# A pre-norm attention and feed-forward kernel: nine bf16 products of constant ones as the warm-up, and the epsilon constant set by GpSimd

## The chip, the core and the metric

The kernel runs on one core of one Trainium2 chip. The metric is the time of one execution in device microseconds, lower is better. The core has a matrix engine (TensorE, PE in the profile; its weight loads are shown apart as PEld), three engines for elementwise work (VectorE or DVE, ScalarE or ACT, GpSimd or POOL), and a queue engine (SyncE, SP) that here issues nearly all DMA transfers.

## What is computed

One transformer block on 2048 tokens of 1024 features: a layer norm, sliding-window attention with 32 heads, a residual, a second layer norm, a SiLU feed-forward of width 3584, a residual. Inputs and output are bf16.

```
def _A_ref(x, wqkv, wo):
    B, S, D = x.shape
    H = 32; Dh = D // H; W = 256
    qkv = (lambda x, *d: x.transpose(*d))((x @ wqkv).reshape(B, S, 3, H, Dh), 2, 0, 3, 1, 4)
    ...
    mask = (idx[:, None] - idx[None, :] >= 0) & (idx[:, None] - idx[None, :] < W)
    ...
def _B_ref(x, w1, w2):
    h = _silu(jnp.einsum("bsd,df->bsf", x, w1))
    return jnp.einsum("bsf,fd->bsd", h, w2)

h = x + _A_ref(_layernorm(x, axis=-1), A_wqkv, A_wo)
h2 = h + _B_ref(_layernorm(h, axis=-1), B_w1, B_w2)
```

## The kernel before

The tokens are worked in four blocks of 512, each block in four tiles of 128 tokens. On-chip memory is cut by hand into a few regions (`r_w` weights and the transposed normed tokens, `r_o` the ring of token tiles, `r_a` queries, keys, values and later activations, `r_e` scratch and the attention probabilities). The order of instructions on each engine is the order in which the program writes them (`tc.manual_schedule()`); the tile framework adds the semaphores. After the opening, TensorE goes through value, query and key products for block 0, then the same products of each later block with the attention of the block before woven in, then the output projection, then the feed-forward. The change touches only the first microseconds, which run as follows.

**Preamble.** GpSimd sets four one-element-per-partition constants of the runtime (line 749 in the profile), among them `const-bfloat16-1.0`; then all engines pass a common start.

**Constants (lines 147 to 153).** VectorE clears `warm`, a 128x128 f32 patch at the start of `r_e`, and sets `eps`, one f32 in each partition. ScalarE's first work is a square root of `eps` into `dummy`; it brings in the table of the square root, and nothing reads its result. Because that instruction reads `eps`, ScalarE's queue stands at it until `eps` is there.

**Loads (lines 155 to 163).** SP issues token tile 0 (`load_x(0, 0)`, 256 KB). ScalarE issues token tile 1 (`load_x(0, 1, nc.scalar)`), right behind the square root in its queue. SP then issues the first 512 value columns of the weights in four parts of 256 KB (`load_wqkv(2 * D, 4)`, line 145; part n holds row blocks 2n and 2n+1 of the eight that a product sums over), then token tiles 2 and 3 and the other columns.

**Identity and ones column (lines 165 to 167).** GpSimd builds `ident`, the 128x128 identity for transposes on TensorE (a memset and an affine select inside `make_identity`), and then sets the column of ones beside the values in `r_a`.

**Warm-up (lines 170 to 176).** TensorE multiplies the zeros of `warm` by themselves, once over 512 and once over 384 columns, in f32, into the bank `o_ps[0]`. Nothing reads the result. Each shows as two weight loads and two products in the trace.

**First tokens (lines 463 to 498).** For tiles 0 and 1, ScalarE takes the mean of one half (`half_mean`, line 467), VectorE that of the other (469); VectorE subtracts the mean (`center`, 474) in four pieces; TensorE transposes pairs of 128x128 pieces (`turn_first`, 224), ScalarE (VectorE for some of tile 1) copies them from PSUM (227), and TensorE multiplies them with the value weights (497). The list `ORDER` fixes the sequence on TensorE: transposes (0,0), (0,1), (0,2) of tile 0, products with row blocks 0 and 1, transpose (0,3), products with row blocks 2 and 3, transpose (1,0), products with 4 and 5, and so on. ScalarE's queue holds the half means of tile 0 and tile 1 first and the copies of the transposes behind them. `eps` is read again by later square roots (lines 215, 482) and by the exponential that brings in its table (544).

Of the kernel before, what the change touches and what calls it, by code (L numbers as in the profile page):

```python
# [8 lines left out]
BF16 = mybir.dt.bfloat16  # L9
F32 = mybir.dt.float32  # L10
# [4 lines left out]
P = 128  # L15
N_HEADS = 32
WINDOW = 256
LN_EPS = 1e-5
# [30 lines left out]
def kernel(  # L49
# [10 lines left out]
    nc = tc.nc  # L60
# [15 lines left out]
    const = ctx.enter_context(tc.tile_pool(name="const", bufs=1))  # L76
# [13 lines left out]
    r_e = big.tile([P, 13312], BF16, name="r_e")  # L90
# [5 lines left out]
    o_ps = [ps.tile([P, 8, 64], F32, name=f"o_ps{i}") for i in range(2)]  # L96
    acc_ps = [ps.tile([P, 512], F32, name=f"acc{i}") for i in range(2)]

    def view(region, off, *dims):
        n = 1  # L100
        for d in dims:
            n *= d
        ap = region[:, off:off + n]
        if len(dims) == 2:
            return ap.rearrange("p (a b) -> p a b", b=dims[1])
        if len(dims) == 3:
            return ap.rearrange("p (a b c) -> p a b c", b=dims[1], c=dims[2])
        return ap
# [35 lines left out]
        for k in range(0, KT, n):  # L144
            queues[k // n % len(queues)].dma_start(out=dst[:, k:k + n, :], in_=wqkv_v[:, k:k + n, c0:c0 + 512])

    warm = view(r_e, 0, 2 * P).bitcast(F32)
    nc.vector.memset(warm, 0.0)

    eps = const.tile([P, 1], F32, name="eps")  # L150
    nc.vector.memset(eps[:], LN_EPS)
    dummy = const.tile([P, 1], F32, name="dummy")
    nc.scalar.activation(out=dummy[:], in_=eps[:], func=ACT.Sqrt)

# [7 lines left out]
            load_x(0, 3)  # L162
    load_wqkv(0)

    ident = const.tile([P, P], BF16, name="ident")
    make_identity(nc, ident[:])
    nc.gpsimd.memset(v[:, :, :, DH:VW], 1.0)


    wide = bass.AP(tensor=warm.tensor, offset=warm.offset, ap=[warm.ap[0], [0, 4], warm.ap[1]])  # L170

    def busy(n):
        nc.tensor.matmul(o_ps[0][:].rearrange("p (a c) b -> p a (c b)", c=2)[:, 0:n], lhsT=warm, rhs=wide[:, 0:n], start=True, stop=True)

    for n in (4, 3):
        busy(n)


    def ln_half(xt, stats, c):
# [399 lines left out]
    for g0 in range(0, G, 4):  # L579
        for w in range(2):  # L580
            for g in range(g0, g0 + 4):
                qk_group(0, w, g, dve if g % 2 else act)
                n = g0 * 2 + w * 4 + g % 4
# [105 lines left out]
    for b in range(NB):  # L689
# [4 lines left out]
        for ft in range(FT):  # L694
# [8 lines left out]
            if b == 0 and 7 <= ft < 15:  # L703
                j, c = divmod(ft - 7, 2)
# [60 lines left out]
```

## Time and profile before

| | us |
|---|---|
| median of three runs | 692.42 |
| the three runs | 692.87, 690.78, 692.42 |
| the profiled execution | 692.34 |
| its span, first to last instruction | 690.5 |
| TensorE busy in the span | 675.9 |
| VectorE, ScalarE, GpSimd busy | 291.8, 244.0, 160.6 |

The span leaves out 692.34 - 690.5 = 1.84 us before the first and behind the last instruction. In a timeline, each line gives start, length, engine, source line, operation, output and input, how many instructions are merged, and in brackets how long the engine sat idle before and what ended that. A product's shown length contains its drain, so the distance from start to start is what a product costs in a row of them.

### The profile page before, as it was taken

What the parts mean: (1) busy time and instruction counts of PE and PEld (TensorE: products, weight loads), DVE (VectorE), ACT (ScalarE), POOL (GpSimd) and SP (SyncE); (2) the same over time, 40 slices, a digit from 0 to 9 for tenths busy, and PEclk for the clock granted to TensorE, in tenths of its full rate; (3) what the DMA queues carried; (4) which work ended last, traced back from release to release, by engine and by line L of the source; (5) the groups of instructions that cost most, each with busy time, mean ns of one, the idle gap of its engine ahead of it and who ended that gap; (6) DMA issues with size and microseconds to landing.
All of it is one profiled execution on the core that took longest, in us unless ns stands there. A gap on an engine that the chain in (4) does not pass through costs nothing.

```text
span 690.5 us, 14116 instructions
## 1 busy us (share of the span) xinstructions
PE 675.9 (98%) x5890; PEld 341.8 (50%) x6004; DVE 291.8 (42%) x614; ACT 244.0 (35%) x465; POOL 160.6 (23%) x295
## 2 busy tenths in 40 slices
PE   9999999999999999999999999999999999999998
PEld 4445555555555555544444444444444444444445
DVE  5267647744444449443316133343133251333111
ACT  6326666666667666421310033300133100233000
POOL 1006666566666656500000000000000000000000
DMA  8832141136241879970023310022300024100110
GB/s 263 270 57 76 39 86 56 25 64 184 72 131 24 257 219 270 229 266 31 32 84 108 92 39 0 1 91 70 85 0 1 24 88 94 39 1 1 30 39 24
DMA packets 78640, 61.48 MB, mean 89 GB/s; under 512 B 52464, under 2 KB 62704, under 8 KB 78576
## 3 DMA queue, kind: packets, MB, share of 16 engines
q1 hardware_dynamic: 78432, 60.31, 31.4%
q8 instruction: 47, 0.77, 0.5%
q10 hardware_dynamic: 144, 0.26, 0.1%
q14 instruction: 17, 0.14, 0.1%
HBM read 39.85 MB, written 8.39 MB: 70 GB/s over the span
## 4 chain that ended last, share of the span: by engine, by line
PE 94%; DMA 2%; DVE 2%; issue 1%; SPq 0%; DVEq 0%
PE hacc L675 19%; PE acc L259 16%; PE hacc L712 14%; PE acc L712 14%; PE acc L675 9%; PE acc L249 6%; PE o_ps L392 5%; PE acc L280 4%; PE sc L312 2%; PE hacc L280 1%; DMA r_a<-h_dram 1%; PE sc L364 1%; DMA h_dram<-r_t 1%; DMA r_w<-in_A_wqkv_dram 1%; DVE ln_st L180 1%
## 5 line engine op out<-in xcount | busy, mean ns | idle before, releaser
L382 POOL TENSOR_SCALAR_AFFINE_SELECT r_e<-r_e 128x512 bf16<-128x512 bf16 (+1 forms) x288 | 157.6, 562 | 125.7 <-ACT r_e L372 61.1
L712 PEld LDWEIGHTS <-r_a 128*128 128x128 bf16 x952 | 90.7, 98 | 103.1
L675 PEld LDWEIGHTS <-r_w 128*128 128x128 bf16 x896 | 87.2, 98 | 105.0
L675 PE MATMUL hacc<-r_e,r_w 128*128 128x512 bf16 x468 | 104.9, 379 | 0.5
L712 PE MATMUL hacc<-r_a 128*128 128x512 bf16 (+1 forms) x496 | 100.2, 361 | 0.4
L324 ACT ACTIVATE r_e<-sc 128x768 bf16<-128x768 f32 x96 | 78.2, 814 | 48.6 <-PE sc L312 46.9
L712 PE MATMUL acc<-r_a 128*128 128x512 bf16 (+1 forms) x439 | 94.5, 373 | 0.5
L684 ACT ACTIVATE r_n<-hacc 128x512 f32<-128x512 f32 x30 | 17.9, 597 | 178.9 <-PE hacc L675 177.8
L259 PEld LDWEIGHTS <-r_w 128*128 128x128 bf16 x512 | 47.1, 98 | 55.0 <-issue 1.0
L261 DVE CAST r_a<-acc 128x512 bf16<-128x512 f32 x56 | 38.7, 691 | 57.4 <-PE acc L259 54.9
L259 PE MATMUL acc<-r_t,r_w 128*128 128x512 bf16 x233 | 56.5, 380 | 2.4 <-issue 1.7
L259 PE MATMUL acc<-r_w 128*128 128x512 bf16 x240 | 56.0, 380 | 1.5 <-issue 1.0
L392 PEld LDWEIGHTS <-r_e 128*128 128x128 bf16 x1440 | 47.4, 96 | 18.0
L280 PE MATMUL acc<-r_o,r_a 128*128 128x512 bf16 x188 | 46.6, 380 | 2.8 <-issue 1.1
L392 PE MATMUL o_ps<-r_a,r_e 128*128 128x33 bf16 x1440 | 48.1, 178 | 0.0
L675 PE MATMUL acc<-r_e,r_w 128*128 128x512 bf16 x191 | 43.3, 379 | 0.2
L727 DVE SCALAR_TENSOR_TENSOR r_t<-acc,r_t 128x512 bf16<-128x512 f32 (+1 forms) x16 | 10.6, 664 | 69.3 <-PE acc L712 69.3
L325 ACT ACTIVATE r_e<-sc 128x256 bf16<-128x256 f32 x96 | 37.6, 392 | 0.0
L280 PEld LDWEIGHTS <-r_a 128*128 128x128 bf16 x256 | 23.4, 98 | 28.2 <-issue 1.6
L685 DVE SCALAR_TENSOR_TENSOR r_a<-r_n,hacc 128x512 bf16<-128x512 f32 x30 | 20.6, 688 | 33.0 <-ACT r_n L684 33.0
L685 DVE SCALAR_TENSOR_TENSOR r_a<-r_a,hacc 128x512 bf16<-128x512 f32 x30 | 20.6, 688 | 31.2 <-ACT r_a L684 31.2
L727 DVE SCALAR_TENSOR_TENSOR r_t<-hacc,r_t 128x512 bf16<-128x512 f32 (+1 forms) x18 | 11.6, 646 | 51.5 <-PE hacc L712 51.5
(104 smaller groups left out, 547.4 us busy)
## 6 DMA issues: line engine op xcount, KB each, us to landing
r_w<-in_B_w_dram SPq DMA_DIRECT2D x8, 896.0 KB, 5.4
r_a<-in_B_w_dram SPq DMA_DIRECT2D x7, 1024.0 KB, 7.2
r_w<-in_A_wqkv_dram SPq DMA_DIRECT2D x4, 1024.0 KB, 8.9
h_dram<-r_t SPq DMA_DIRECT2D x16, 256.0 KB, 2.9
r_t<-h_dram SPq DMA_DIRECT2D x16, 256.0 KB, 2.8
out_dram<-r_t SPq DMA_DIRECT2D x31, 128.0 KB, 1.7
r_o<-in_A_x_dram SPq DMA_DIRECT2D x15, 256.0 KB, 4.2
r_e<-h_dram SPq DMA_DIRECT2D x3, 1024.0 KB, 5.5
```

The lines of the kernel that those rows point to most:

```text
L249: nc.tensor.matmul(acc, lhsT=lnT_b[b % 2][:, kt, j * P:(j + 1) * P], rhs=wv[:, kt, c * 512:(c + 1) * 512], start=(kt == 0), stop=(kt == KT ...
L259: nc.tensor.matmul(acc, lhsT=wqk[:, kt, col0:col0 + P], rhs=lnT_b[b % 2][:, kt, :], start=(kt == 0), stop=(kt == KT - 1))
L261: copy(out=(qT, kT)[which][b][:, g, :], in_=acc)
L280: nc.tensor.matmul(acc, lhsT=qT[b][:, g, j * P:(j + 1) * P], rhs=wo[:, g, c * 512:(c + 1) * 512], start=(g == 0), stop=(g == G - 1))
L324: nc.scalar.activation(out=tri[:, :, :, 64:256], in_=both, func=ACT.Exp, scale=scale)
L325: nc.scalar.activation(out=e[:, 1024:1280].rearrange("p (h q) -> p h q", q=P), in_=bank[:, :, 192:320], func=ACT.Exp, scale=scale)
L382: nc.gpsimd.affine_select(out=dst, in_=src, pattern=[[0, n] for n in dst.shape[1:-1]] + [[sgn, P]], compare_op=ALU.is_ge if upper else ALU ...
L392: nc.tensor.matmul(o_ps[pair][:, qt * 2 + hh, 0:VW], lhsT=chunk_of(i, bank, piece, pair, hh), rhs=v[:, b * 4 + kt, g * 4 + pair * 2 + hh, ...
L675: nc.tensor.matmul(acc, lhsT=w1[:, kt, ft * P:(ft + 1) * P], rhs=ln2T[b][:, kt, :], start=(kt == 0), stop=(kt == KT - 1))
L685: nc.vector.scalar_tensor_tensor(out=gT[:, ft, :], in0=th, scalar=1.0, in1=acc, op0=ALU.add, op1=ALU.mult)
L712: nc.tensor.matmul(acc[:, 0:c1 - c0], lhsT=gT[:, ft, j * P:(j + 1) * P], rhs=w2[ft // 4][:, ft % 4, c0:c1], start=(ft == 0), stop=(ft == F ...
L727: nc.vector.scalar_tensor_tensor(out=t_out[j % 2][:, c0:c1], in0=acc[:, 0:c1 - c0], scalar=0.5, in1=t_in[j % 2][:, c0:c1], op0=ALU.mult, o ...
```

## The change

The zeroed patch `warm`, its VectorE memset and the two f32 products are gone. In their place stand nine bf16 products of the runtime's constant one, spread by step 0 to 128 weight columns and 512 moving columns, into the same bank. The identity moves up in the program, ahead of `eps`, and `eps` is set by GpSimd instead of VectorE; so on GpSimd's queue come the two instructions of the identity, then `eps`, then the column of ones.

```
-    warm = view(r_e, 0, 2 * P).bitcast(F32)
-    nc.vector.memset(warm, 0.0)
-
+    ones = nc.const_aps.tensor_like(1.0, r_e[:, 0:512])
+    for n in range(9):
+        nc.tensor.matmul(o_ps[0][:].rearrange("p a b -> p (a b)"), lhsT=ones[:, 0:P], rhs=ones, start=True, stop=True)
+
+    ident = const.tile([P, P], BF16, name="ident")
+    make_identity(nc, ident[:])
     eps = const.tile([P, 1], F32, name="eps")
-    nc.vector.memset(eps[:], LN_EPS)
+    nc.gpsimd.memset(eps[:], LN_EPS)
     dummy = const.tile([P, 1], F32, name="dummy")
     nc.scalar.activation(out=dummy[:], in_=eps[:], func=ACT.Sqrt)
...
-    ident = const.tile([P, P], BF16, name="ident")
-    make_identity(nc, ident[:])
     nc.gpsimd.memset(v[:, :, :, DH:VW], 1.0)
 
-
-    wide = bass.AP(tensor=warm.tensor, offset=warm.offset, ap=[warm.ap[0], [0, 4], warm.ap[1]])
-
-    def busy(n):
-        nc.tensor.matmul(o_ps[0][:].rearrange("p (a c) b -> p a (c b)", c=2)[:, 0:n], lhsT=warm, rhs=wide[:, 0:n], start=True, stop=True)
-
-    for n in (4, 3):
-        busy(n)
```

## The prediction

> **What bounds the kernel now.** I read the page's busy shares first, then the chain of waits over the first 8 us, then the timeline of TensorE and of ScalarE there. The page says that TensorE is the bound, and that it is full in every slice but the last:
>
> ```profile
> PE 675.9 (98%) x5890; PEld 341.8 (50%) x6004; DVE 291.8 (42%) x614; ACT 244.0 (35%) x465; POOL 160.6 (23%) x295
> PE   9999999999999999999999999999999999999998
> ```
>
> So the change can only move the moment from which TensorE runs without a pause; whatever comes later follows that moment rigidly. The chain of waits of the first 8 us (start, length, what) shows what sets it:
>
> ```profile
> 0.80 0.40 SPq L139
> 1.20 0.06 issue
> 1.26 0.41 SPq L145
> 1.67 0.05 issue
> 1.72 5.12 DMA r_w<-in_A_wqkv_dram
> 6.84 0.04 issue
> 6.88 0.59 PE acc L497 x2
> 7.47 0.11 PE tp L224 x2
> 7.58 0.02 issue
> 7.60 0.59 PE acc L497 x2
> ```
>
> The chain goes through no warm-up, no identity and no `eps`. It is SP's issues, then the landing of the second part of the value weights at 6.84. I take 7.60 as the second gate: the pair of products there needs the third part, and the two transposes ahead of it have left the array by about 7.31 + 2 x 0.055 = 7.42 (0.055 is half of the 0.11 that two take in the chain), so some 0.18 us went to waiting. From 7.60 on TensorE's pieces touch. The timeline of TensorE and then of ScalarE:
>
> ```profile
> 1.12 3.35 PE L173 MATMUL o_ps<-r_e 128*128 128x512 f32 x4 [1.12 <-DVE eps L151]
> 4.82 0.91 PE L224 MATMUL tp<-ident,r_e 128*128 128x128 bf16 x6 [0.35 <-DVE r_e L474]
> 5.58 1.04 PE L497 MATMUL acc<-r_w 128*128 128x512 bf16 x2
> 6.41 0.39 PE L224 MATMUL tp<-ident,r_e 128*128 128x128 bf16 x2
> ...
> 1.13 0.42 ACTq L139 DMA_DIRECT2D r_o<-in_A_x_dram  x1
> 2.09 0.20 ACT L153 ACTIVATE dummy<-eps 128x1 f32<-128x1 f32 x1
> ...
> 4.47 0.63 ACT L467 ACTIVATE r_e<-r_o 128x512 bf16<-128x512 bf16 x1
> 5.00 0.19 ACT L467 ACTIVATION_READ_ACCUMULATOR r_e<-r_o 128x1 f32 x1
> 5.26 0.99 ACT L227 COPY r_w<-tp 128x128 bf16<-128x128 bf16 x4
> ```
>
> The reader should see three things. The warm-up ends at 4.47 and TensorE then waits 0.35 us for VectorE's centred tokens, so it is not what the transposes wait for. ScalarE's issue of token tile 1 starts at 1.13, just behind the `eps` of VectorE. And ScalarE works on tile 1 (4.47) before it copies the first transposes (5.26).
>
> **The change, part by part.**
>
> *Zeros and f32 products removed.* VectorE loses 0.17 us (clearing `warm`) and 0.06 us (`eps`), both before 1.07; its next work waits for token tile 0 until 3.61, which hides them: nothing. TensorE loses a stretch from 1.12 to 4.47.
>
> *Nine products added.* They wait for nothing inside the program, since the constant is set before the common start. SP and ScalarE begin at 0.80 and VectorE at 0.90, so I let the products begin at 0.9. The trace has no bf16 product of step-0 operands. The nearest row is the pair of line 497 at 5.58, where the clock was still low: two products take 1.04 us, the second alone 0.63, so they start 1.04 - 0.63 = 0.41 us apart; at the later, fast clock six take 1.46 with 0.38 for the last, (1.46 - 0.38) / 5 = 0.216 apart, and twice that is 0.43. I take 0.43: 9 x 0.43 = 3.9 us, ending near 4.8, when the centred tokens come (4.82). The weight loads lie inside the products, as at 5.98, where one of 0.15 us starts with a product. Lower end: the fast clock comes in between, they end sooner and TensorE waits as before: nothing. Upper end with loads not hidden: 9 x (0.43 + 0.15) = 5.2, ending at 6.1. The upper end by the row of f32 products, 0.85 for one (the 384-column ones; 1.06 to 1.22 for 512), is a rival below.
>
> What does a late end cost? From the first transpose to the products at 7.60 the work needs, at the fast clock: 0.76 to the first product (4.82 to 5.58), then 0.216, 0.216, two transposes 0.11, 0.216, 0.216, 0.11, together 1.85 us. So the warm-up may end as late as 7.60 - 1.85 = 5.75 free of charge. An end at 4.8 costs nothing; one at 6.1 costs 0.35.
>
> *`eps` on GpSimd.* Before, `eps` was done at 1.01 + 0.06 = 1.07. GpSimd's select of the identity starts at 1.07 and its next instruction at 1.31; a 128x1 memset of GpSimd takes 0.10 (four in the preamble). So `eps` is done at 1.41, 0.34 later. Queued behind the square root on ScalarE is the issue of tile 1: 1.13 becomes 1.47. The square root itself started at 2.09 behind its table load, which hides the delay. The column of ones (2.32 us on GpSimd) shifts by about 0.1; it ended at 3.63, and ScalarE writes the first values beside it at 14.26: nothing.
>
> *Tile 1 later.* It landed a median of 3.3 us after its issue, at 1.13 + 3.3 = 4.43, and ScalarE's second half mean began at 4.47: that DMA is what it waited for, and the delay comes through in full. With the same 3.3 it lands at 4.77, and ScalarE is free for copies at 5.19 + 0.34 = 5.53 and not 5.26: +0.27. The first product goes to 5.85, the second to 6.26, the two transposes at the low clock need until 6.9 (5.58 to 6.41 took 0.83; add 0.22 for two), and the pair of 6.88 starts at about 6.92: +0.04, which the second gate's 0.18 swallows. VectorE meets tile 1 at 5.45, later than 4.77, and needs ScalarE's half of the mean at 6.24, later than 5.53. Cost: nothing.
>
> Bounds: SP's first weights (issued 1.26) may now be served ahead of tile 1. 256 KB at the 306 GB/s of the stretch 5 to 6 us is 0.86 us, so tile 1 could land at 5.3, copies slip by 0.8, and at the low clock the first product comes at 6.4, the second at 6.8, the transposes are through at 7.4, and two products and two transposes more (0.54) reach the second gate near 8.0, 0.4 late. The other way, weights served ahead of tile 1 by the same 0.86 would land sooner, but TensorE waits only some 0.4 us in all before 7.60 (0.25 ahead of 6.88, 0.18 ahead of 7.60): -0.4 at most, and only if ScalarE's copies came in time, which a late tile speaks against. I take 0. The Trainium skill ("DMA: Bandwidth & Descriptors", Queues, rings and completion order) says each DMA engine goes round between queues with work, one packet at a time. By that, tile 1 from ScalarE's queue and the weights from SP's would share, and tile 1 would land between 4.8 and 5.3; the sum by it would be +0 to +0.4, against 0 by the row.
>
> *Sum:* 0 + 0 + 0 + 0.04 - 0.04 = 0, against the profiled execution's 690.5 + 1.84 = 692.34. That stands 0.08 below the median of 692.42, so I forecast 692.4, and move it to 692.5 because the open ends of the last two parts all point to later.
>
> **The rivals.**
>
> *Tile 1 lands late and the cover is too small.* For: ScalarE starts on it within 0.04 us of the landing, and the copies sit behind. Against: two gates by weights follow. +0.4: 692.8.
>
> *Slower: the step-0 products are long.* If one takes as long as the 384-column f32 row, 0.85, nine end at 0.9 + 7.7 = 8.6. The transposes start at 8.6 and not 4.82, the gate of 7.60 is reached at 8.6 + 1.85 = 10.45: +2.85, 695.2. It begins to cost at (5.75 - 0.9) / 9 = 0.54 us a product. For: no row shows a matrix operand with step 0 in both places. Against: the rows of plain bf16 give 0.43 at worst.
>
> *The clock rises later.* A weight load takes 0.15 at 6.51 and 0.10 at 6.88, and products shrink from 0.63 to 0.38: before, the clock rose between these, 5.4 to 5.8 us after the first f32 product. Counted so from 0.9 it rises at 6.3 to 6.7, as before. If the ones did not count and the count began with the work at 4.82, it would rise at 10.2 to 10.6; every microsecond at the low clock behind 7.60 does half a microsecond's work, so (10.6 - 7.6) / 2 = 1.5: 693.8. Against: nine products without a gap fill more of the time than what they replace. By the Trainium skill ("TensorE: Matmul & The Clock Gate", What's actually happening) the clock follows a free-running window of about 3.4 us of activity; an estimate from it is a rise between 4.3 and 7.7, so at most 0.05 us lost. The trace agrees as far as one rise can show.
>
> *Faster.* A clock that is up at 4.8 gains nothing, as both gates are landings. Only sooner landings help; the whole wait from 6.41 + 0.22 to 6.88 and the 0.18 at the second gate make some 0.4: 692.0. More than that must come from what the trace of one execution does not show; one of the three runs took 690.78.
>
> **How the numbers follow.** About 0.3%, 2.1 us, is what a measurement of this kernel can tell from no change; the three runs before differ by as much. Forecast 0.50 (0.44 within, 0.03 to each side for scatter of the runs). Late tile 0.17 (0.15 within, 0.02 slower). Long products 0.13 (0.04 within, 0.09 slower). Late clock 0.10 (0.05 within, 0.05 slower). Sooner, or a cause unseen 0.10 (0.02 within, 0.08 faster). Together: faster 0.11, within 0.70, slower 0.19. The range goes from 690.6, just under the fastest run before, to 694.6, which takes in the late clock and the lower half of the long products.
>
> **What would show it.** Right: nine products start near 0.9, 0.43 apart, end by 4.9; ScalarE's issue starts near 1.47; its second half mean near 4.8; the chain still goes through a landing near 6.84 and the pair at 7.6 moves by less than 0.4. Wrong: products more than 0.54 apart, a second half mean after 5.3, low-clock products behind 7.6, or a move of the span with the pair at 7.6 unmoved, which would mean that the change reached something behind the opening.

## The result, and the profile after

The changed kernel takes 700.74 us, the median of four runs (700.32 to 702.49); the kernel before took 692.30 in the same comparison. The ratio over all the runs is 1.014, with a 95% interval of 1.0119 to 1.016 (the two medians alone give 1.012): 1.4% slower, where no change was forecast. The profiled execution of the changed kernel took 701.02 with a span of 699.2, against 690.5 before.

The page's busy line and its slices of 17.5 us each (TensorE's busy tenths, the granted TensorE clock in tenths) put the loss in the first slice:

```profile
PE 678.3 (97%) x5894; PEld 342.9 (49%) x6009; DVE 292.0 (42%) x612; ACT 243.9 (35%) x465; POOL 160.6 (23%) x296
PE   4999999999999999999999999999999999999998
PEclk7999999999999999999999999999999999999999
```

TensorE's busy time grew by 2.4 us (675.9 to 678.3), the span by 8.7. The rest is a hole at the start, and the clock fell in it. The chain of waits of the first 20 us names what made the hole:

```profile
0.81 0.40 SPq L139
...
1.73 4.80 DMA r_w<-in_A_wqkv_dram
6.54 0.02 issue
6.55 6.25 DMA r_o<-in_A_x_dram
12.80 0.02 issue
12.83 0.02 ACTq L460
12.84 0.05 issue
12.89 0.72 ACT r_e L460 x2
13.62 0.16 ACT r_w L220
13.78 0.05 issue
13.82 1.03 PE acc L490 x2
```

A landing of weights at 6.54 releases an issue at 6.55; that issue is the load of a token tile, which takes until 12.80; ScalarE takes its half mean, copies, and the first product starts at 13.82 where it started at 5.58. ScalarE's timeline shows whose issue it is:

```profile
2.09 0.20 ACT L156 ACTIVATE dummy<-eps 128x1 f32<-128x1 f32 x1
6.55 0.38 ACTq L139 DMA_DIRECT2D r_o<-in_A_x_dram  x1
6.99 0.63 ACT L460 ACTIVATE r_e<-r_o 128x512 bf16<-128x512 bf16 x1 [4.69 <-DMA r_w<-in_A_wqkv_dram]
7.52 0.19 ACT L460 ACTIVATION_READ_ACCUMULATOR r_e<-r_o 128x1 f32 x1
12.89 0.63 ACT L460 ACTIVATE r_e<-r_o 128x512 bf16<-128x512 bf16 x1 [5.19 <-DMA r_o<-in_A_x_dram]
13.43 0.18 ACT L460 ACTIVATION_READ_ACCUMULATOR r_e<-r_o 128x1 f32 x1
13.52 0.96 ACT L220 COPY r_w<-tp 128x128 bf16<-128x128 bf16 x4
```

The square root of `eps` runs at 2.09, as before the change, so `eps` itself was in time. The issue of token tile 1 stands right behind it in ScalarE's queue and goes out at 6.55 instead of 1.13. Everything behind it waits too: the half mean of tile 0, whose data lay there since 3.7, starts at 6.99 with 4.69 us of idle time that the profile puts down to a landing in `r_w`, the weights. ScalarE has no use for weights there; the only thing that the two share is a counter. The compiled programs, as listed with the waits of each instruction, say so (ScalarE's queue, before and after, in my abbreviation):

```
before:  Activation dummy<-eps        [waits DVE]
         DMACopy r_o<-in_A_x_dram
after:   Activation dummy<-eps        [waits Pool]
         DMACopy r_o<-in_A_x_dram     [waits DMAHW2]
```

The framework hands its DMA transfers eight completion counters, DMAHW0 to 7, in turn, in the order in which it plans them. The ninth transfer gets the counter of the first, and its issue first waits until that first transfer has landed. Before, tile 1 was planned fourth (counter 3). After, all ten of SP's first transfers are planned ahead of it, the last two of them with waits on counters 0 and 1; tile 1 is eleventh, gets counter 2, and that is the second part of the value weights. The experiments below test this.

TensorE's timeline gives the rest:

```profile
0.84 4.00 PE L149 MATMUL o_ps<-const-bfloat16-1.0 128*128 128x512 bf16 x9 [0.84 <-PEq L742]
8.14 0.91 PE L217 MATMUL tp<-ident,r_e 128*128 128x128 bf16 x6 [3.31 <-DVE r_e L467]
13.82 1.03 PE L490 MATMUL acc<-r_w 128*128 128x512 bf16 x2 [4.77 <-ACT r_w L220]
```

The nine products (x9; a product starts every 0.43 us) do what was forecast for them, 0.84 to 4.84. Then come pauses of 3.31 and 4.77 us. The table by stretches (TensorE busy, its weight loads, VectorE, ScalarE, GpSimd, each with the count; granted clock; DMA share; GB/s) shows the clock after them:

```profile
5.00:10.00 5.00, 0.91 (x6) 0.36 (x6) 1.11 (x4) 0.72 (x2) 0.00 (x0) 0.86 1.00 320
10.00:15.00 5.00, 1.18 (x5) 0.71 (x6) 1.88 (x7) 1.59 (x6) 0.00 (x0) 0.50 1.04 346
15.00:20.00 5.00, 5.00 (x22) 2.42 (x21) 2.07 (x6) 2.76 (x7) 0.00 (x0) 0.61 0.03 11
20.00:25.00 5.00, 4.95 (x30) 2.46 (x29) 4.14 (x11) 3.28 (x9) 0.00 (x0) 1.00 0.00 0
```

A mean of 0.61 over 15 to 20 is half clock for (1 - 0.61) / 0.5 x 5 = 3.9 us: TensorE runs at half speed until about 18.9, five microseconds into its dense work. The trace's own clock records, of which these means are made, have full clock from 5.22 to 8.63 and half clock from there to 18.87. Ahead of its first record a trace says nothing of the clock, and the column then reads 1.00 all the same: the nine products start 0.43 us apart, twice the 0.216 of the fast clock, under a column of 1.00. Where records are missing, the spacing of the products decides.

**Where the 8.7 us lie.** Compare the same instruction in both traces. ScalarE's second half mean is 12.89 - 4.47 = 8.42 us late, the first product 13.82 - 5.58 = 8.24. The exponential that brings in its table (line 544 before, 537 after) starts at 20.06 before and 29.84 after: 9.78 late, so the lag grows by 1.54 while the clock is low (the kernel before had a short stretch of low clock there too). The end of the span is 8.7 late: 1.1 is made good on the way. That part is in the output projection; the waits of TensorE between 255 and 310 us, before and then after, show it:

```profile
PE acc L280 <- DVE r_t L282: 1.0, 2, 0.6
```

```profile
PE acc L273 <- DVE ln_t L195: 0.2, 1, 0.2
```

Before, TensorE waited there twice for VectorE's residual sums, 1.0 us in all; after it waited 0.2. Other traces have more or less of this wait whatever the opening does (none in the run with `eps` ahead of the identity, 0.9 and 0.3 in the run with 46 products), so I count it to the scatter. The trace of before is thus one of the longer executions of its kernel: in the later comparisons the kernel before gave medians of 690.46 to 691.14, and the changed kernel again 701.06, about 10 us more, which is nearer to the lag of 9.78 than to the 8.7.

### The profile page after: what moved, and what is told of

It is laid out like the page before. It is cut to its first block, busy times and chain, and to the rows that moved or that the text cites. A ratio compares the mean times of both kernels' runs of the same rounds, so it can differ in the third digit from the quotient of the medians.

```text
span 699.2 us, 14124 instructions
## 1 busy us (share of the span) xinstructions
PE 678.3 (97%) x5894; PEld 342.9 (49%) x6009; DVE 292.0 (42%) x612; ACT 243.9 (35%) x465; POOL 160.6 (23%) x296
## 4 chain that ended last, share of the span: by engine, by line
PE 96%; DMA 2%; issue 1%; ACT 0%; SPq 0%; DVE 0%; ACTq 0%
PE hacc L668 19%; PE acc L252 16%; PE hacc L705 14%; PE acc L705 13%; PE acc L668 8%; PE acc L273 6%; PE acc L242 6%; PE o_ps L385 5%; PE sc L305 2%; PE hacc L273 1%; DMA r_o<-in_A_x_dram 1%; PE sc L357 1%; DMA r_w<-in_A_wqkv_dram 1%; PE sc L331 1%; PE o_ps L242 0%
```

## The experiments

Theory A: tile 1's issue waits for a completion counter that it shares with a weights transfer, because it is planned eleventh. Theory B: the nine products, or the clock behind them, cost the time. Theory C: GpSimd's `eps` is late for ScalarE by itself.

**One half alone.** First the changed kernel with `eps` back on VectorE, then the kernel before with only the identity and `eps` moved.

```
-    nc.gpsimd.memset(eps[:], LN_EPS)
+    nc.vector.memset(eps[:], LN_EPS)
```

> The changed kernel with one line put back: VectorE sets eps; the nine products of ones and the early identity stay. Theory A (a completion counter: with eps behind the identity on GpSimd, token tile 1's transfer is planned eleventh, shares a completion counter with the second part of the value weights, and its issue waits for that landing): here its issue waits for no landing, starts near 1.13 us, the second half mean near 4.5, and the time is 692.3, within 1 us. Theory B (the nine products or their clock cost the time): 700 to 701 as in the changed kernel. Theory C (GpSimd's eps is itself late for ScalarE): 692.3, too.

```
+    ident = const.tile([P, P], BF16, name="ident")
+    make_identity(nc, ident[:])
     eps = const.tile([P, 1], F32, name="eps")
-    nc.vector.memset(eps[:], LN_EPS)
+    nc.gpsimd.memset(eps[:], LN_EPS)
...
-    ident = const.tile([P, P], BF16, name="ident")
-    make_identity(nc, ident[:])
```

> The kernel before with the other half alone: identity ahead, eps on GpSimd behind it, but the two f32 products of zeros as before (VectorE still clears their patch). Theory A and theory C: 700 to 701.5, with the issue of tile 1 near 6.5 us. Theory B: 692.3.

The first took 690.75 us, ratio 0.9999 (0.999 to 1.0009); the second 700.36, ratio 1.014 (1.0125 to 1.0155). The kernel before gave 691.14 beside them, so the 692.3 that was expected of the first is met as a ratio and not as a time. ScalarE's issue in the first, and in the second:

```profile
0.97 0.38 ACTq L139 DMA_DIRECT2D r_o<-in_A_x_dram  x1
```

```profile
6.30 0.38 ACTq L139 DMA_DIRECT2D r_o<-in_A_x_dram  x1
6.73 0.63 ACT L467 ACTIVATE r_e<-r_o 128x512 bf16<-128x512 bf16 x1 [4.45 <-DMA r_w<-in_A_wqkv_dram]
```

The whole loss is with `eps`, and none with the products. Theory B falls.

**The same GpSimd, earlier in its queue.** The changed kernel with the two lines of the identity behind `eps`.

```
+    eps = const.tile([P, 1], F32, name="eps")
+    nc.gpsimd.memset(eps[:], LN_EPS)
     ident = const.tile([P, P], BF16, name="ident")
     make_identity(nc, ident[:])
-    eps = const.tile([P, 1], F32, name="eps")
-    nc.gpsimd.memset(eps[:], LN_EPS)
```

> The changed kernel with GpSimd setting eps ahead of the identity. Theory A: the transfer of tile 1 is planned early again and gets a counter of its own; issue at 1.0 to 1.1 us, time 692.3 within 1 us. Theory C: a wait of ScalarE for GpSimd remains, so most of the 8.4 us remains: above 698.

690.80 us, ratio 1.000 (0.9987 to 1.0013), issue at 0.94. GpSimd now sets `eps` at 0.80 where it did at 1.31, half a microsecond of real time, and 10 us of run time go. Theory C cannot make that of it.

**The counter, step by step.** These two leave `eps` behind the identity on GpSimd and take transfers away from ahead of tile 1. One fewer, by loading tiles 2 and 3 together:

```
-    load_x(0, 2)
+    nc.sync.dma_start(out=view(r_o, 2048, 2, 1024), in_=x2d[2 * P:4 * P, :].rearrange("(j p) d -> p j d", p=P))
     for k in (0, 4):
         nc.sync.dma_start(out=wv[:, k:k + 4, 512:1024], in_=wqkv_v[:, k:k + 4, 2 * D + 512:3 * D])
-        if k == 0:
-            load_x(0, 3)
```

> The changed kernel with token tiles 2 and 3 loaded by one transfer of 512 KB instead of two, so one transfer fewer is planned ahead of tile 1; eps stays on GpSimd behind the identity. Theory A: tile 1 is now the tenth transfer, its counter is that of the first part of the value weights, so its issue follows that landing near 4.3 us instead of 6.5; about 2.2 us of the loss come back: 698.5 within 1. Theory C (GpSimd's eps late by itself): the issue stays near 6.5 and the time at 700 to 701.

Three fewer, with this beside it:

```
-    load_wqkv(2 * D, 4)
+    for k0, k1 in ((0, 2), (2, 4), (4, 8)):
+        nc.sync.dma_start(out=wv[:, k0:k1, 0:512], in_=wqkv_v[:, k0:k1, 2 * D:2 * D + 512])
...
-    for k in (0, 4):
-        nc.sync.dma_start(out=wv[:, k:k + 4, 512:1024], in_=wqkv_v[:, k:k + 4, 2 * D + 512:3 * D])
+    nc.sync.dma_start(out=wv[:, :, 512:1024], in_=wqkv_v[:, :, 2 * D + 512:3 * D])
```

> The changed kernel with seven transfers ahead of tile 1 instead of ten (tiles 2 and 3 in one, value weights of the first columns in parts of 256, 256 and 512 KB, those of the second columns in one of 1 MB); eps stays on GpSimd behind the identity. Theory A: tile 1 is the eighth transfer and has a counter of its own, so its issue waits only for eps, near 1.47 us, and tile 1 lands near 4.8. The larger transfers land later as a whole, which costs 0.5 to 2.5 us by itself: 691.5 to 694.5. Theory C: 700 to 701.

ScalarE's timeline of the first of them, and of the second:

```profile
4.40 0.37 ACTq L139 DMA_DIRECT2D r_o<-in_A_x_dram  x1
...
11.69 0.63 ACT L458 ACTIVATE r_e<-r_o 128x512 bf16<-128x512 bf16 x1 [6.14 <-DMA r_o<-in_A_x_dram]
```

```profile
1.44 0.38 ACTq L139 DMA_DIRECT2D r_o<-in_A_x_dram  x1
...
5.05 0.63 ACT L458 ACTIVATE r_e<-r_o 128x512 bf16<-128x512 bf16 x1 [0.70 <-DMA r_o<-in_A_x_dram]
```

With one transfer fewer the issue follows the landing of the first weights part, at 4.40; with three fewer it goes out at 1.44, as soon as `eps` is there. `eps` was set by the same instruction in the same place each time, so theory A stands and theory C falls. The times were 699.44 us (1.0124, 1.0107 to 1.0141) and 693.63 (1.0051, 1.0036 to 1.0067). The first returned less than the 2.2 us that I expected. The issue came 6.55 - 4.40 = 2.15 sooner, but the half mean only 12.89 - 11.69 = 1.20: from issue to landing the transfer took 7.20 us in the chain of waits, against 6.25. By then most of SP's first loads are under way beside it; in the table above the DMA engines are full from 10 to 15, with a share of 1.04. The second pays for its large weights transfers, as expected: TensorE's chain there goes through their landing at 10.06, and the pair of products that needs it starts at 10.11 where it started at 7.60, 2.5 us late. In these waits the clock fell as well: half clock is recorded from 10.20 to 13.61, which costs half of 3.4 us more.

**The issue taken out from behind `eps`.** Two ways: ScalarE issues tile 1 ahead of its square root, or SP issues it.

```
+    load_x(0, 1, nc.scalar)
     nc.scalar.activation(out=dummy[:], in_=eps[:], func=ACT.Sqrt)
...
-    load_x(0, 1, nc.scalar)
```

> The changed kernel with ScalarE's issue of tile 1 moved ahead of its square root of eps; eps stays on GpSimd behind the identity. Theory A and theory C: issue near 0.8 us, tile 1 lands 0.3 us sooner than before the change, the square root's table load 0.4 us later, time 692.0 within 1 us. Theory B: 700 to 701.

```
-    load_x(0, 1, nc.scalar)
+    load_x(0, 1)
```

> The changed kernel with token tile 1 issued by SP as its second transfer instead of by ScalarE; eps stays on GpSimd behind the identity. Theory A: the issue no longer stands behind eps in the plan, tile 1 is the second transfer with a counter of its own, and the loss goes: 690.5 to 692, no different from the kernel before. Theory C: ScalarE's square root still waits for GpSimd, but nothing stands behind it until 3.6 us, so the same.

692.89 us (1.0022, 1.0009 to 1.0036) and 691.28 (1.0007, 0.9997 to 1.0017). In both the loss is gone or nearly so, as A says; C expects the same here, so they add nothing between these two. What I had wrong is the sooner landing in the first. The tiles 0 and 1 were issued at the same moment, and both came later for it:

```profile
0.80 0.40 ACTq L139 DMA_DIRECT2D r_o<-in_A_x_dram  x1
...
4.75 0.63 ACT L460 ACTIVATE r_e<-r_o 128x512 bf16<-128x512 bf16 x1 [2.03 <-DMA r_o<-in_A_x_dram]
```

The half mean of tile 0 begins at 4.75 and not at 3.61. The 0.33 us by which `eps` held back tile 1 in the kernel before let tile 0 through alone. The clock takes its share as well: TensorE's timeline there has products 0.41 to 0.43 us apart, and the trace records full clock only from 9.91 on:

```profile
5.96 0.91 PE L217 MATMUL tp<-ident,r_e 128*128 128x128 bf16 x6 [1.12 <-DVE r_e L467]
6.71 1.04 PE L490 MATMUL acc<-r_w 128*128 128x512 bf16 x2
...
8.82 1.06 PE L490 MATMUL acc<-r_w 128*128 128x512 bf16 x2
```

Beside the trace of before, the lag is 6.71 - 5.58 = 1.13 us at the first product and 21.83 - 20.06 = 1.77 at the exponential. With tile 1 issued by SP the record of full clock begins at 6.06. That the pause of 1.12 us behind the nine products is what made the clock late is likely, but no run tests it.

**The clock.** The changed kernel with 46 products instead of 9, beside the changed kernel once more.

> The changed kernel with 46 products of ones instead of 9. They run until about 13 us, just ahead of ScalarE's first copy at 13.5, so TensorE has no pause in which the clock could fall. If the low clock behind the pause makes the lag grow from 8.25 to 9.78 us between the first copy and 20 us, the growth of 1.5 us goes and the time is 1.5 us under the changed kernel's, 699.2. If the growth has another cause, the time stays at 700 to 701.

> The changed kernel itself, beside the three others on one chip: 1.0119 to 1.016 of the kernel before, as measured.

699.64 us (1.0134, 1.0119 to 1.0149) against 701.06 (1.0152, 1.0137 to 1.0167): 1.4 less, where 1.5 was expected, though the two intervals overlap. The table by stretches for 46 products, beside that of the changed kernel above:

```profile
10.00:15.00 5.00, 3.73 (x24) 1.94 (x23) 1.73 (x7) 1.70 (x7) 0.00 (x0) 1.00 1.06 356
15.00:20.00 5.00, 5.00 (x33) 2.46 (x32) 3.56 (x11) 3.59 (x9) 0.00 (x0) 1.00 0.06 22
```

The clock stays at 1.00, and 33 products and transposes fit between 15 and 20 where 22 did. So the pause cost twice: the wait itself, and the half clock behind it. How much the second part is, the times tell less well than the traces. From the first product to the exponential it is 29.84 - 13.82 = 16.02 us in the changed kernel and 27.70 - 14.14 = 13.56 with 46 products: 2.5 us sooner, about half of the five at half clock. The execution traced with 46 products then lost some of this in the output projection, where it waited 0.9 and 0.3 us for residual sums. That the medians differ by just the 1.5 expected is therefore luck in part.

**What the warm-up is worth.** With `eps` on VectorE, the nine products are left out.

> The changed kernel with eps by VectorE and no warm-up products at all: what the nine products are worth when tile 1 is on time. If the clock rises 5.4 to 5.8 us after TensorE's first work, which is then the transposes near 5.2, it rises near 10.8, and half of the stretch from 7.5 is lost: about 1.6 us over the kernel with the nine products, ratio to the kernel before 1.002. If the products are worth nothing: 1.000.

692.40 us, 1.0026 (1.0015 to 1.0037). Beside the ratio of 0.9999 with the nine products this is about 0.3%, or 1.9 us. The time is as expected, but the reckoning behind it was not: it had the clock rise near 10.8, and the trace has full clock recorded from 9.16 on, by which the same reckoning gives only (9.16 - 7.5) / 2 = 0.8 us. So nine bf16 products of ones do what the f32 products of zeros did; no version tried was faster than the kernel before.

## Why the prediction failed

- **What bounds the kernel**: right. TensorE is rigid behind the opening; the lag of 9.78 at 30 us stands unchanged until the output projection.
- **Nine products**: right. Forecast from 0.9, 0.43 apart, to 4.8; measured 0.84 to 4.84. The rival of long products is gone with them. So is that of a clock that the ones do not raise: with 46 of them, full clock is recorded from 3.90 on, while nothing else had run on TensorE.
- **`eps` on GpSimd**: right in itself. Forecast done at 1.41, and the trace has it at 1.31 + 0.10.
- **"So `eps` is done at 1.41, 0.34 later. Queued behind the square root on ScalarE is the issue of tile 1: 1.13 becomes 1.47."** This step failed: it became 6.55. I took the issue's only wait to be the one on `eps` that I could see in the code. The instruction that waits on `eps` moved in the framework's plan, with it the issue behind it, and with the plan's order went the counter. The runs with the tenth and eighth place (4.40 and 1.44) show that 5.1 of the 5.4 us of delay are the counter's. The term put at nothing on this ground is the whole loss, 8.24 us at the first product.
- **"With the same 3.3 it lands at 4.77."** This failed because the step before it did. Where the issue did go out at 1.44, in the run with the eighth place, the transfer took 3.5 us and ScalarE's half mean started at 5.05, inside the stated bounds of 4.77 and 5.3 (with larger weights parts beside it). Issued at 6.55, with SP's ten loads put out before it, it took 6.25 and landed at 12.80.
- **The rival of the late tile** had the right place and the right chain (ScalarE's half mean, the copies, the first product), at 0.4 us instead of 8.2.
- **The clock**: I priced a late rise from too little warm-up, and forecast it at 6.3 to 6.7 from one trace. Full clock is recorded from 5.22 here, and from 6.06 and 6.13 in two runs with tile 1 on time, so the warm-up sufficed. What came instead was a fall behind it, in the stretch with the pause, by which the lag grew 1.54 us.

The trace of before held a hint that I did not use. Its table of waits of SP's queue (who waited for what; total us, times, longest) has this line in the first 30 us:

```profile
SPq L145 <- DMA r_w<-in_A_wqkv_dram: 1.4, 1, 1.4
```

An issue of weights waits for an earlier landing of weights in the same region, though the two write different columns: nothing but a shared counter asks for that.

## What to carry to other kernels

A transfer issued from a compute engine's queue sits behind that engine's waits twice: in time, and in the plan from which a framework deals out its few completion counters. Before changing what such an engine waits for first, list the waits of every DMA issue behind it, in the compiled program before and after; a wait on a counter that the source does not mention is the thing to look for. In this kernel the constant that ScalarE's first instruction reads did no harm when it stood first in its engine's queue (690.80), nor did the early load when SP issued it (691.28). By what rule the framework orders its plan was not examined.

## What the runs showed of the hardware

- Two loads of 256 KB issued together from two queues delay each other: the first half mean, on the first of them, began at 4.75 with both issued at 0.80, at 3.95 to 4.12 with 0.13 to 0.17 us between them (three runs), and at 3.61 with 0.33.
- A load of 256 KB issued by 1.44 took 3.3 to 3.8 us to land (six traces); issued at 4.40 or later, with most of SP's first loads put out before it, it took 6.18 to 7.20 (five traces).
- The clock fell without any pause of 3.4 us. Three traces record full clock for 3.41 us and then half clock: from 5.22 to 8.63 in the changed kernel, from 4.43 to 7.84 with the tenth place, from 6.78 to 10.20 with the eighth. TensorE was busy for 0.49, 1.07 and 1.10 us of these stretches, and the longest pause up to the fall was 3.31, 1.28 and 1.59 us. Half clock then lasted for 10.24, 10.25 and 3.41 us, three times 3.41 or once. The Trainium skill ("TensorE: Matmul & The Clock Gate", HAM oscillation) gives as its abstract rule that no idle gap may exceed about 3.4 us; taken as a rule for a single gap, these traces do not bear it out. They look like a decision every 3.41 us on how busy the stretch was; that is argued from three falls and not tested.
- Without any warm-up full clock is recorded from 9.16 on, 3.8 us after the first transpose at 5.35, sooner than the 5.4 to 5.8 that I had read from the kernel before. With the nine products it is first recorded from 4.43 to 6.78 in five traces, and from 9.91 in that with the issue ahead. So the time of the rise is not a constant that one trace gives.
